# Three subtractions on GpSimd, written in a loop of their own that follows the arrival of batch 2's x

## The chip, the core and the metric

The kernel runs on one core of one Trainium2 chip. The metric is the device time of one execution in microseconds. The kernel before took 658.3 us (median of three runs, 654.86 to 660.84). The profile is of one further execution.

## The reference

All is in float32. Batches B = 4, heads H = 12, sequence S = 448, head size D = 64.

```
scores = q @ k.T / sqrt(64) - log(448)
attn   = sigmoid(scores)
x      = (attn @ v), heads side by side        # 1792 x 768
y      = ((x @ w_a) * (x @ w_b)) @ w_out       # 1792 x 1536, then 1792 x 768
logits = y @ phi                               # 8 experts of 4 slots
d      = softmax of logits over the tokens     # slot_input = d.T @ y
per expert: relu(slot_input @ w1) @ w2
out    = softmax of logits over the slots @ slot_out
```

## The kernel before, in words

**Attention** goes by pairs of heads, six to a batch: pair g is pair g % 6 of batch g // 6 (batches are counted from 0), 24 in all. For a pair VectorE (DVE) turns k and q, rounds each to a high part and subtracts that for a low part (`emit_TK`: transpose, cast, subtraction for k, then the same three for q; L205, L197, L198). TensorE (PE) makes the scores from these parts (L260: high by high, high by low, low by high), ScalarE (ACT) the sigmoid (L266), PE the product with v (L288, L294, L301), and ACT or DVE copies the result out as x of the pair (L323), `xt[g]`. From pair 14 on the pairs are finished two by two: the x of 14 and 15 are copied out one after the other, then those of 16 and 17.

**The first expert layer** is x @ w_a times x @ w_b. Batch 0 and batch 3 go by `ab`. Batches 1 and 2 go together as the two block rows of a Strassen product (Winograd's form, `unit`, L879): A11 and A12 are the first and last three x tiles of batch 1, A21 and A22 those of batch 2. For each of the three tiles i the operands are made in place: S3 = A11 - A21 (L800), S1 = A21 + A22 (L801), S2 = A22 - S3 (L802), S4 = A12 - S2 (L807, L812). A11 itself, A12 and S2 are also split into high and low parts (`split_x`, L782, L783). S3, S1, A22 and S4 are split later (`late_operands`), when the attention is over.

**The weights** of these products are read back from DRAM: `load_u(0)` (L737) reads the first block into the tile hp0, `prep_u(0)` makes the weight blocks from it. Its first step, `block(0, 0)`, is a cast on DVE (L754) and a subtraction on GpSimd (POOL, L755); the next ones are four subtractions on POOL (L768, L770).

**What sets the order.** Each engine runs its instructions in the order in which they are written, and the order is made by generators that are advanced by turns. The loop at the end of attention advances `att_g`; at each of its steps it advances `ops = operands()` once. What `operands` yields decides on the weights: if it yields 1 and the x of pair 15 is there, or if it has ended, `prep_u(0)` is advanced by a step:

```
        if next(ops, 0) in ((0, 1) if GQ + 1 in xt else (0,)):
            pu = pu or prep_u(0)
            next(pu, None)
```

`load_u(0)` is written when the x of pair 13 is there. All reads from DRAM go through the queue of SyncE (SP), in order.

Of the kernel before, what the change touches and what calls it, by code (L numbers as in the profile page):

```python
# [14 lines left out]
ALU = mybir.AluOpType  # L15
# [12 lines left out]
NP = H // 2  # L28
# [13 lines left out]
def body(ctx, tc, q, k, v, w_a, w_b, w_out, phi, w1, w2, out):  # L42
    nc = tc.nc
    pe, act, dve, pool, sp = nc.tensor, nc.scalar, nc.vector, nc.gpsimd, nc.sync
# [259 lines left out]
    xt = {}  # L304
# [475 lines left out]
    def split_x(nm, i, t, pl, names, rnd=None, sub=None):  # L780
        xh, xl = (pl.tile([128, S], F32R, tag=x, name=x) for x in names)
        (rnd or dve.tensor_copy)(xh, t)  # L782
        (sub or pool).tensor_tensor(xl, t, xh.bitcast(F32), op=ALU.subtract)  # L783
        xs[nm, i] = xh, xl

    def operands():

        cp, late = pools["cp"], []
        for i in range(3):
            split_x("A11", i, xt[NP + i], cp, (f"A11h{i}", f"A11l{i}"), act.copy)  # L790
            yield
            split_x("A12", i, xt[NP + 3 + i], cp, (f"A12h{i}", f"A12l{i}"), act.copy)
            yield
        for i in range(3):
            while 2 * NP + 3 + i not in xt:
                yield 1
            yield
            a11, a12, a21, a22 = (xt[n + i] for n in (NP, NP + 3, 2 * NP, 2 * NP + 3))
            s2 = cp.tile([128, S], F32, tag="s2", name="s2", bufs=2)
            pool.tensor_tensor(a11, a11, a21, op=ALU.subtract)  # L800
            pool.tensor_tensor(a21, a21, a22, op=ALU.add)  # L801
            pool.tensor_tensor(s2, a22, a11, op=ALU.subtract)  # L802
            for _ in range(5):
                yield
            split_x("S2", i, s2, cp, (f"S2h{i}", f"S2l{i}"))
            if not i:
                pool.tensor_tensor(a12, a12, s2, op=ALU.subtract)  # L807
            else:
                late.append((a12, s2))
            yield  # L810
        for a12, s2 in late:
            pool.tensor_tensor(a12, a12, s2, op=ALU.subtract)  # L812
# [391 lines left out]
    for kk in range(NP):  # L1204
# [6 lines left out]
    pools["cp"] = cp_ctx.enter_context(tc.tile_pool(name="cp", bufs=1, side="left"))  # L1211
    run["lsd2"] = (hps_t[0][:, 1536:1536 + S], hps_t[1][:, 1536:1536 + S], hps_t[2][:, 4 * S:4 * S + 128], hps_t[2][:, 4 * S + 128:])
    ops, pu = operands(), None
    then = [(2 * NP + 1, lambda: load_u(0)), (GQ + 5, lambda: reload_gk(0, 1, gk_01[1])),
            (GQ + 6, lambda: load_u(1)), (GQ + 7, lambda: reload_gk(0, 0, gk_01[0])),
# [234 lines left out]
```

## Time and profile before

| | |
|---|---|
| three runs | 658.3 us median, 654.86 to 660.84 |
| profiled execution | 654.76 us, span 652.9 us |
| PE busy | 626.5 us (96%) |
| DVE / ACT / POOL busy | 383.6 / 298.3 / 310.1 us |
| stretch of the change | 215 to 280 us of the span, the last pairs of attention |

Times in rows are microseconds from the span's start, unless marked ns. A row of the timeline gives the start, the duration, the engine, the line, the operation with output and inputs, and in brackets the time that the engine sat idle before it and what ended that. PE's ends are modelled. The granted clock is TensorE's, as a share of full speed.

### The profile page before, as it was taken

How to read it: one execution, taken by the hardware profiler on the slowest of the kernel's cores; microseconds unless marked ns; L12 is line 12 of the kernel's file. 1: busy time of each engine (PE TensorE's matmuls, PEld its weight loads, DVE VectorE, ACT ScalarE, POOL GpSimd, SP SyncE). 2: the span in 40 equal slices, each digit the busy share in tenths (PEclk: the TensorE clock that was granted, in tenths of full speed). 3: DMA queues.
4: the chain of work that ended last, by engine and by line, in shares of the span. 5: the costliest groups of instructions: out<-in, count | busy, mean ns of one | idle time of the engine just before them, and what ended most of it. 6: DMA issues, size and time to landing. Idle time of an engine off the chain costs nothing.

```text
span 652.9 us, 10851 instructions
## 1 busy us (share of the span) xinstructions
PE 626.5 (96%) x3989; PEld 447.6 (69%) x3989; DVE 383.6 (59%) x557; ACT 298.3 (46%) x539; POOL 310.1 (47%) x235
## 2 busy tenths in 40 slices
PE   8999999999999999999999999999999999997685
PEld 5557777777776554489988989887889885441121
DVE  4764877889793789498677776856243323030013
ACT  4988889889875876754423332201110002110012
POOL 0234587777772267379986576553335431000000
PEclk9999999999999999999999999999999999998899
DMA  9999889799878766901314333299899999999998
GB/s 213 268 275 261 274 284 340 260 301 301 256 177 209 139 148 125 276 19 49 97 50 105 102 100 84 71 261 319 230 380 405 392 329 367 419 401 416 410 372 300
DMA packets 148564, 159.76 MB, mean 245 GB/s; under 512 B 73584, under 2 KB 126640, under 8 KB 144432
## 3 DMA queue, kind: packets, MB, share of 16 engines
q1 hardware_dynamic: 145984, 157.35, 77.2%
q10 hardware_dynamic: 2528, 1.72, 0.8%
q8 instruction: 32, 0.52, 0.3%
q14 instruction: 20, 0.16, 0.1%
HBM read 129.11 MB, written 29.93 MB: 244 GB/s over the span
## 4 chain that ended last, share of the span: by engine, by line
PE 74%; DMA 16%; ACT 3%; DVE 3%; issue 2%; SPq 1%; ACTq 0%; POOL 0%; DVEq 0%; POOLq 0%
PE ab L686 24%; PE sc L879 16%; PE ab L879 8%; PE sc L260 6%; PE sc L288 5%; DMA misc<-clog 3%; DMA eb<-in_moe_w 2%; DMA e<-in_moe_w 2%; DMA hp<-in_moe_w 2%; DMA hp<-ab 2%; PE ab L294 2%; ACT a L266 1%; PE ms L600 1%; DMA ea<-in_moe_w 1%; PE ms L213 1%
## 5 line engine op out<-in xcount | busy, mean ns | idle before, releaser
L472 POOL TENSOR_TENSOR w<-gk,cy 128x768 int32<-128x768 int32 x36 | 66.3, 1843 | 70.8 <-DVE gk L460 39.7
L266 ACT ACTIVATE a<-sc,sums 112x448 f32<-112x448 f32 (+1 forms) x149 | 84.1, 649 | 13.1 <-PE sc L260 13.1
L686 PE MATMUL ab<-t,wh 128*128 128x448 f32 x288 | 64.6, 370 | 0.1
L693 ACT COPY misc<-ab 128x448 f32<-128x448 f32 x24 | 12.7, 529 | 100.4 <-PE ab L686 100.4
L686 PEld LDWEIGHTS ab<-t,wh 128*128 128x128 f32 x288 | 53.5, 188 | 6.8 <-issue 1.8
L570 POOL TENSOR_TENSOR wl<-w,wh 128x768 fp32r<-128x768 f32 x24 | 46.2, 1928 | 10.9 <-ACT wh L569 10.9
L570 POOL TENSOR_TENSOR wl<-hp,wh 128x768 fp32r<-128x768 f32 x16 | 29.4, 1840 | 42.2 <-DVE wh L569 15.3
L288 PE MATMUL sc<-a,vn 112*64 112x448 f32 x192 | 38.7, 545 | 0.2 <-ACT a L266 0.2
L696 DVE TENSOR_TENSOR misc<-misc,ab 128x448 f32<-128x448 f32 x24 | 14.7, 611 | 36.6 <-PE ab L686 36.5
L458 DVE TENSOR_SCALAR mf<-gk 128x768 f32<-128x768 f32 x24 | 22.7, 944 | 22.9 <-ACT gk L441 22.9
L686 PE MATMUL ab<-xh,wl 128*128 128x448 f32 x144 | 34.8, 377 | 0.0
L686 PE MATMUL ab<-xh,wh 128*128 128x448 f32 x144 | 34.5, 375 | 0.0
L754 ACT CAST wx<-T 128x384 fp32r<-128x384 f32 x19 | 9.7, 512 | 53.9 <-DVE T L776 35.9
L686 PE MATMUL ab<-t,wl 128*128 128x448 f32 x144 | 34.3, 373 | 0.0
L686 PE MATMUL ab<-xl,wh 128*128 128x448 f32 x144 | 34.0, 371 | 0.0
L1409 DVE COPY o<-sc 128x384 f32<-128x384 f32 x10 | 5.4, 554 | 48.5 <-PE sc L1387 47.4
L260 PE MATMUL sc<-qh,kh 64*112 64x448 f32 (+1 forms) x139 | 32.2, 432 | 1.0 <-ACT qh L197 0.6
L755 POOL TENSOR_TENSOR wx<-hp,wx 128x384 fp32r<-128x384 f32 x27 | 31.6, 1173 | 2.2 <-ACT wx L754 2.1
L686 PEld LDWEIGHTS ab<-xh,wh 128*128 128x128 f32 x144 | 26.0, 188 | 7.3 <-issue 4.7
L686 PEld LDWEIGHTS ab<-xl,wh 128*128 128x128 f32 x144 | 26.4, 188 | 5.5 <-issue 3.5
L686 PEld LDWEIGHTS ab<-t,wl 128*128 128x128 f32 x144 | 26.7, 188 | 5.1 <-issue 2.0
L686 PEld LDWEIGHTS ab<-xh,wl 128*128 128x128 f32 x144 | 25.7, 188 | 5.1 <-issue 1.7
(511 smaller groups left out, 1574.6 us busy)
## 6 DMA issues: line engine op xcount, KB each, us to landing
hp<-ab SPq DMA_DIRECT2D x14, 768.0 KB, 4.5
gk<-gk SPq DMA_DIRECT2D x44, 224.0 KB, 4.3
ab<-w SPq DMA_DIRECT2D x24, 384.0 KB, 6.9
eb<-in_moe_w SPq DMA_DIRECT2D x7, 1024.0 KB, 11.9
ea<-in_moe_w SPq DMA_DIRECT2D x7, 1024.0 KB, 11.6
eb<-in_moe_w SPq DMA_DIRECT2D x7, 768.0 KB, 15.1
ea<-in_moe_w SPq DMA_DIRECT2D x7, 768.0 KB, 15.0
wr_cv<-in_moe_w_a SPq DMA_DIRECT2D x6, 768.0 KB, 7.9
```

The source lines that it names most:

```text
L260: pe.matmul(sc[h], kx[r, cs], qx[r], start=(i == 0), stop=(i == 2))
L266: act.activation(a, sc, AF.Sigmoid, bias=nlog[:n], scale=1.0 / math.sqrt(D))
L288: pe.matmul(pv[64 * h:64 * h + 64], qkv_t["v", g][:, h, c, :], a_t.pop((g, h, c)), start=(c == 0), stop=(c == C - 1))
L294: pe.matmul(pv[64 * h:64 * h + 64], qkv_t["v", g][:, h, c], a_t.pop((g, h, c)), start=(c == 0), stop=False)
L458: dve.tensor_scalar(mf, m, LOW, HIGH, op0=ALU.max, op1=ALU.min)
L472: pool.tensor_tensor(thirds(w), m.bitcast(I32), thirds(cy_t.pop(x)), op=ALU.add)
L570: pool.tensor_tensor(wl, t, wh.bitcast(F32), op=ALU.subtract)
L686: pe.matmul(t, w[:, kk * 128:(kk + 1) * 128], xt[b * NP + kk][xi], start=(s == 0 and kk == 0), stop=(s == 2 and kk == KD - 1))
L693: act.copy(gT_all[n % 5], t)
L696: dve.tensor_tensor(g, g, t, op=ALU.mult)
L755: pool.tensor_tensor(w[:, 1], t, w[:, 0].bitcast(F32), op=ALU.subtract)
L879: pe.matmul(t, w[:, wi, k * 128:(k + 1) * 128], xs[ORDER[m], k][xi], start=(s == 0 and k == 0), stop=(s == 2 and k == 2))
```

## The change

The subtraction S3 = A11 - A21 is taken out of the loop over the three row blocks and written in a loop ahead of it. That loop waits for the x of pairs 12, 13 and 14, one per turn, where the loop behind it waits for pairs 15, 16 and 17. The new loop yields 1 while it waits and after each subtraction.

```
         for i in range(3):
+            while 2 * NP + i not in xt:
+                yield 1
+            pool.tensor_tensor(xt[NP + i], xt[NP + i], xt[2 * NP + i], op=ALU.subtract)
+            yield 1
+        for i in range(3):
             while 2 * NP + 3 + i not in xt:
                 yield 1
             yield
             a11, a12, a21, a22 = (xt[n + i] for n in (NP, NP + 3, 2 * NP, 2 * NP + 3))
             s2 = cp.tile([128, S], F32, tag="s2", name="s2", bufs=2)
-            pool.tensor_tensor(a11, a11, a21, op=ALU.subtract)
             pool.tensor_tensor(a21, a21, a22, op=ALU.add)
             pool.tensor_tensor(s2, a22, a11, op=ALU.subtract)
```

PE, ACT and SP keep their order. On POOL, at the end of the splits of A11 and A12, there stood before (t0 to t2 are the A11 tiles, hp2 holds A21, misc A22, hp0 the weights):

```order
L800 TENSOR_TENSOR t0_964<-t0_964,hp2_2474 128x448
L801 TENSOR_TENSOR hp2_2474<-hp2_2474,misc_95 128x448
L802 TENSOR_TENSOR s2_2857<-misc_95,t0_964 128x448
L783 TENSOR_TENSOR S2l0_2928<-s2_2857,S2h0_2927 128x448
L807 TENSOR_TENSOR t3_1791<-t3_1791,s2_2857 128x448
L755 TENSOR_TENSOR wl0_2947<-hp0_2472,wl0_2947 128x384
```

and now:

```order
L797 TENSOR_TENSOR t0_964<-t0_964,hp2_2474 128x448
L797 TENSOR_TENSOR t1_1231<-t1_1231,hp2_2474 128x448
L797 TENSOR_TENSOR t2_1513<-t2_1513,hp2_2474 128x448
L755 TENSOR_TENSOR wl0_2851<-hp0_2472,wl0_2851 128x384
L805 TENSOR_TENSOR hp2_2474<-hp2_2474,misc_95 128x448
L806 TENSOR_TENSOR s2_2878<-misc_95,t0_964 128x448
L783 TENSOR_TENSOR S2l0_2948<-s2_2878,S2h0_2947 128x448
L811 TENSOR_TENSOR t3_1791<-t3_1791,s2_2878 128x448
```

The three differences stand together, and the weight subtraction of `block(0, 0)` has moved from behind S4 to a place ahead of S1.

On DVE, from the copy of pair 15's x on, there stood before (kn and qn are k and q of pair 18, then of pair 19):

```order
L323 COPY misc_95<-ab_2829 128x448
L205 STREAM_TRANSPOSE kn_2646<-kn_2646 128x448
L197 CAST kh_2874<-kn_2646 128x448
L198 TENSOR_TENSOR kl_2875<-kn_2646,kh_2874 128x448
L205 STREAM_TRANSPOSE qn_2656<-qn_2656 128x448
L197 CAST qh_2886<-qn_2656 128x448
L198 TENSOR_TENSOR ql_2887<-qn_2656,qh_2886 128x448
L782 CAST S2h0_2927<-s2_2857 128x448
L754 CAST wl0_2947<-hp0_2472 128x384
L205 STREAM_TRANSPOSE kn_2726<-kn_2726 128x448
```

and now:

```order
L323 COPY misc_95<-ab_2831 128x448
L754 CAST wl0_2851<-hp0_2472 128x384
L205 STREAM_TRANSPOSE kn_2647<-kn_2647 128x448
L197 CAST kh_2882<-kn_2647 128x448
L198 TENSOR_TENSOR kl_2883<-kn_2647,kh_2882 128x448
L205 STREAM_TRANSPOSE qn_2657<-qn_2657 128x448
L197 CAST qh_2894<-qn_2657 128x448
L198 TENSOR_TENSOR ql_2895<-qn_2657,qh_2894 128x448
L782 CAST S2h0_2947<-s2_2878 128x448
L205 STREAM_TRANSPOSE kn_2728<-kn_2728 128x448
```

The cast of the first weight block has moved from behind the six steps of pair 18 to a place ahead of them. The reason is in the yields: by the time of the third subtraction the x of pair 15 is there, so the 1 that follows it advances `prep_u(0)` by its first step.

## Rows read from the trace of the kernel before

**Rows 1.** Page, part 4: the chain that ended last, share by engine.

```profile
PE 74%; DMA 16%; ACT 3%; DVE 3%; issue 2%; SPq 1%; ACTq 0%; POOL 0%; DVEq 0%; POOLq 0%
```

**Rows 2.** Windows: us, busy of each engine, granted clock, DMA share, GB/s.

```profile
275.00:300.00 25.00, 25.00 (x211) 21.01 (x208) 20.19 (x26) 13.54 (x31) 18.08 (x15) 1.00 0.16 50
```

**Rows 3.** Waits of PE, 225 to 653 us: in total, times, longest.

```profile
PE ms L260 <- DVE ql L198: 0.6, 1, 0.6
PE ms L260 <- DVE qh L197: 0.4, 1, 0.4
```

**Rows 4.** Timeline of POOL.

```profile
215.12 1.14 POOL L800 TENSOR_TENSOR t<-t,hp 128x448 f32<-128x448 f32 x1
...
230.76 1.16 POOL L801 TENSOR_TENSOR hp<-hp,misc 128x448 f32<-128x448 f32 x1 [14.50 <-DVE misc L323]
231.88 1.30 POOL L802 TENSOR_TENSOR s<-misc,t 128x448 f32<-128x448 f32 x1
...
238.01 1.15 POOL L755 TENSOR_TENSOR wl<-hp,wl 128x384 fp32r<-128x384 f32 x1
...
256.54 2.79 POOL L812 TENSOR_TENSOR t<-t,s 128x448 f32<-128x448 f32 x2
```

**Rows 5.** Timeline of PE.

```profile
235.72 0.37 PE L260 MATMUL ms<-qh,kh 64*128 64x448 f32 x2
...
236.13 0.37 PE L260 MATMUL ms<-ql,kh 64*128 64x448 f32 x2
...
247.20 0.54 PE L260 MATMUL ms<-qh,kh 64*128 64x448 f32 x2 [0.18 <-ACT a L266]
...
248.60 0.54 PE L260 MATMUL ms<-ql,kh 64*128 64x448 f32 x2 [0.65 <-DVE ql L198]
...
259.73 0.54 PE L260 MATMUL ms<-qh,kh 64*128 64x448 f32 x2 [0.35 <-DVE qh L197]
...
260.30 0.53 PE L260 MATMUL ms<-ql,kh 64*128 64x448 f32 x2
...
278.22 0.87 PE L879 MATMUL sc<-S2h,wh 128*128 128x448 f32 x3
```

**Rows 6.** Timeline of SP's queue.

```profile
229.38 0.59 SPq L737 DMA_DIRECT2D hp<-ab  x1
...
449.41 0.87 SPq L1151 DMA_DIRECT2D ea<-out  x1
```

**Rows 7.** Line L737, 215 to 272 us: who waited, and landing.

```profile
  DVE wl L754: 0.3, 1
DMA to landing us min/median/max: 6.5/6.9/7.2
```

**Rows 8.** Timeline of DVE.

```profile
230.00 0.62 DVE L323 COPY misc<-ab 128x448 f32<-128x448 f32 x1 [2.62 <-PE ab L301]
230.54 0.63 DVE L205 STREAM_TRANSPOSE kn<-kn 128x448 f32<-128x448 f32 x1
...
234.68 0.63 DVE L198 TENSOR_TENSOR ql<-qn,qh 128x448 fp32r<-128x448 f32 x1
...
235.92 1.13 DVE L754 CAST wl<-hp 128x384 fp32r<-128x384 f32 x1 [0.31 <-DMA hp<-ab]
236.97 0.63 DVE L205 STREAM_TRANSPOSE kn<-kn 128x448 f32<-128x448 f32 x1
...
242.88 0.65 DVE L205 STREAM_TRANSPOSE kn<-kn 128x448 f32<-128x448 f32 x1 [0.25 <-DMA kn<-in_k]
...
247.09 1.45 DVE L198 TENSOR_TENSOR ql<-gk,qh 128x448 fp32r<-128x448 f32 x1
...
265.99 0.35 DVE L754 CAST wl<-hp 128x384 fp32r<-128x384 f32 x1
```

**Rows 9.** Windows in the last stretch, columns as in rows 2.

```profile
592.20:595.50 3.30, 1.36 (x6) 0.14 (x2) 0.00 (x0) 0.00 (x0) 0.00 (x0) 1.00 1.03 420
595.50:598.80 3.30, 2.75 (x14) 0.57 (x18) 0.00 (x0) 0.00 (x0) 0.00 (x0) 0.53 1.01 411
```

More of the change, by code (lines that the diff above doesn't have):

```diff
@@ L794, in operands @@
         for i in range(3):
+            while 2 * NP + i not in xt:
+                yield 1
+            pool.tensor_tensor(xt[NP + i], xt[NP + i], xt[2 * NP + i], op=ALU.subtract)
+            yield 1
+        for i in range(3):
             while 2 * NP + 3 + i not in xt:
@@ L799, in operands @@
             s2 = cp.tile([128, S], F32, tag="s2", name="s2", bufs=2)
-            pool.tensor_tensor(a11, a11, a21, op=ALU.subtract)
             pool.tensor_tensor(a21, a21, a22, op=ALU.add)
```

## The prediction, made before the changed kernel ran

> **What bounds the kernel now.** I read the chain of waits first: it is PE for 74% and DMA for 16% of the span [rows 1]. The DMA share lies in the last stretch, where expert weights stream in; the change is far ahead of it. The windows come second: right behind the change, where the Strassen products run, PE is busy 25.00 of 25 us [rows 2]. Here the reader should see that a microsecond which PE loses ahead of 275 us has nowhere to be made up in that stage. Then the waits of PE: between 225 us and the products it waits only in the scores of two pairs, for DVE's q parts [rows 3], 0.65 and 0.35 us, with 0.18 us for ACT ahead of the first [rows 5]. So near the change the bound is PE, with DVE close behind it, and POOL far from it. POOL ends its operand work at 256.54 + 2.79 = 259.33 [rows 4], and the first product that reads an S2 starts at 278.22 [rows 5], 18.9 us later. An earlier end of that work is worth nothing by itself.
>
> **The change part by part.**
>
> *The three differences.* As many instructions as before. The first already ran at 215.12, behind the splits, and POOL then stood for 14.50 us [rows 4]; its place in POOL's order is unchanged. The second and third go into that idle time and into the time until the cast below. Each is about 1.14 us [rows 4], and it is taken out of the time behind the cast below, in which POOL runs beside DVE. On the path they cost nothing; the cover is POOL's idle time, and were that gone, the 18.9 us of slack behind it. What they may give is a share of the waits of PE for DVE; it is in the last term.
>
> *The weight block's cast.* This is the part that matters. The new loop's third yield is a 1, and the x of pair 15 is there by then, so DVE's cast of hp0 is written directly behind the copy of x 15, ahead of the six steps that make k and q of pair 18. The cast reads what SP fetches at 229.38 [rows 6], 6.5 us to landing [rows 7], which is 235.9; in the profile it starts at 235.92, after DVE had already waited 0.31 us for that very transfer [rows 8]. SP's order is unchanged and the read is issued from there, so it lands at the same moment in the new kernel. DVE then finishes the copy at 230.62 and stands until 235.92. Queued behind the cast are pair 18's six steps, then S2's cast, then pair 19's. On POOL the subtraction of this block waits for the cast too, and S1 and S2 of the first block behind it; they have the slack named above. ACT has a short copy of pair 18's k in its order, which needs only the first of the six steps; its sigmoids behind it are late, but PE is later.
>
> The cast itself is short when POOL stands: 0.35 us against 1.13 beside POOL [rows 8]. Pair 18's steps therefore begin at 235.92 + 0.35 = 236.27 in place of 230.54. They took 234.68 + 0.63 - 230.54 = 4.77 us, with POOL beside them from 230.76 to 231.88 + 1.30 = 233.18 [rows 4, 8]. Pair 20's, with POOL beside them all the time, took 247.09 + 1.45 - 242.88 = 5.66 [rows 8]. In the new order POOL has three operations beside pair 18's, 1.15 + 1.16 + 1.30 = 3.6 us [rows 4] in place of two. Between 4.77 and 5.66 I take 4.9, nearer the row of the same pair. They end at 241.17. PE's first scores of pair 18 stand at 235.72, and it takes the low part of q at 236.13 [rows 5], 0.82 us after it was ready. Now it gets it at 241.17: PE is late by 241.17 - 236.13 = **5.0 us** (4.9 to 5.8 by the two ends).
>
> *TensorE's clock.* The nearest row for what follows such a stand is in the last stretch: after 3.30 us with 1.36 busy, the granted clock of the next 3.30 us was 0.53 [rows 9], so the work ran at 1.2 GHz for most of them in place of 2.4. Here PE does nothing at all for about 4.5 us before the score matmuls go on. I take it that the clock falls: 3.30 x 0.47 = **1.5 us** more in a stretch where PE always has work. The ends are 0 (the clock holds) and 1.55.
>
> The Trainium skill (TensorE: Matmul & The Clock Gate, Part 1: The HAM clock gate) says that an idle array is put back to 1.2 GHz and gets 2.4 GHz again only after it was kept busy. By that rule the sum holds the 1.5 us; by the short waits of this stretch alone, at which the clock stayed full, it would not. The last stretch of this trace [rows 9] agrees with the page.
>
> *What is won back.* PE's later waits are for DVE, and DVE has less to do there: the cast and its wait (0.31 + 1.13 us [rows 8]) are gone from behind pair 18, and the 0.25 us for k of pair 20 [rows 8] too, since that transfer is long in. From 235.72 to 236.13, undisturbed, the two steps take 0.41 us; from 247.20 to 248.60 they took 1.40, and 0.18 us stood ahead [rows 5]: 0.99 + 0.18 = 1.17 us lost. From 259.73 to 260.30 it is 0.57, so 0.16 + 0.35 = 0.51 [rows 5]. Together 1.7 us; with PE late and slow I take all of it as won back (**-1.7 us**); with none, 0.
>
> *The sum.* 5.0 + 1.5 - 1.7 = **+4.8 us**. Behind that, PE's work and the loads are paced alike: the first expert load is issued at 449.41 [rows 6], by steps that PE's products set, so the shift is carried to the end. Against the profiled execution (654.76 us) that is 659.6. This execution lies 3.5 us under the median of the three runs, 658.3, and against the median the sum is **663.1 us**.
>
> **Rivals.**
>
> 1. *The clock holds.* Then the 1.5 us are not paid, but PE meets DVE sooner and wins back only about 1.2 of the 1.7: 5.0 - 1.2 = +3.8, so 662.1. For it: PE ran through short waits at full clock here. Against it: [rows 9], with PE at least partly busy before the fall.
>
> 2. *Nothing is won back and pair 18 is slow.* 5.8 + 1.5 = +7.3, so 665.6. DVE stays as far behind as PE, so that the two later waits stay where they are. For it: DVE's six steps beside POOL need 5.66 us, and PE's pairs follow each other at (247.20 - 235.72) / 2 = 5.7 [rows 5]. Against it: DVE loses 1.4 us of work in just that place.
>
> 3. *Faster: the read is there in time.* Each microsecond by which hp0 lands sooner than 235.92 takes one off PE's stand; from 235.92 - 5.0 = 230.9 on there is none. Then only the relief is left: DVE runs pair 20's and 22's steps with two POOL operations fewer beside them and PE gets back up to 1.7 us, 656.6. For it: nothing in SP's order forbids a quicker transfer. Against it: 6.5 us is the shortest of the two reads of this line in this stretch [rows 7], and it would have to take 1.5.
>
> 4. *The stand is there, but the end does not move.* The last stretch waits for DMA; if the weight stream began at its old time, PE's lateness would be taken up in waits there: +0, 658.3. Against it: 449.41 [rows 6] is a step in PE's program, and PE is full up to it [rows 2].
>
> 5. *The change does less than it says.* For the first of the three differences that is so: nothing moves. It changes neither sum nor chance.
>
> **Chances.** Forecast 0.50, the clock holds 0.17, nothing won back 0.15, the end does not move 0.10, faster 0.06; 0.02 for what I do not see. About 1% is what three runs of this kernel can tell, since those shown lie 0.9% apart. 1% of 658.3 is 6.6 us, so that the forecast (+0.7%) counts as no change unless the runs scatter upwards. Slower by over 1% holds most of rival 2 and a quarter of the forecast, 0.25; faster by over 1% would need 6.6 us that no part gives, 0.03; within 1% is 0.72. The range goes from 656 (rival 3, and the end that does not move) to 668 (rival 2 with the scatter of the runs): it leaves out about 2 in 10.
>
> **What would show it.** In the new profile: on DVE the cast from hp0 straight behind the copy of pair 15's x, with some 5 us idle before it, ended by the read of hp0; pair 18's steps ending near 241; on PE one wait for DVE's q part of pair 18, about 4.5 to 5 us, the longest of attention, and a low granted clock in the 3 us behind it; the waits of 0.65 and 0.35 us gone; the first product of S2, 278.22 before [rows 5], near 283. On POOL the second and third difference near 219 and 231. I am wrong if DVE's idle time before the cast is under 1 us, if PE does not wait there, or if the products begin late and the end does not.

## The result and the profile after

The changed kernel took 659.95 us (median of 21 runs, 657.73 to 664.57), the kernel before 657.05 us (21 runs, 653.82 to 660.84). The ratio is 1.0053, 95% interval 1.0039 to 1.0066: slower by 3.5 us (2.6 to 4.3), inside 1%. The prediction was 663.1 us against 658.3, which is +4.8; range 656 to 668. The profiled execution has a span of 658.1 us against 652.9.

DVE after the copy of pair 15's x, columns as in [rows 8], which it answers:

```profile
230.75 0.62 DVE L323 COPY misc<-ab 128x448 f32<-128x448 f32 x1 [2.53 <-PE ab L301]
236.01 0.36 DVE L754 CAST wl<-hp 128x384 fp32r<-128x384 f32 x1 [4.64 <-DMA hp<-ab]
236.29 0.64 DVE L205 STREAM_TRANSPOSE kn<-kn 128x448 f32<-128x448 f32 x1
...
240.44 0.63 DVE L198 TENSOR_TENSOR ql<-qn,qh 128x448 fp32r<-128x448 f32 x1
240.98 0.39 DVE L782 CAST S2h<-s 128x448 fp32r<-128x448 f32 x1
241.28 0.64 DVE L205 STREAM_TRANSPOSE kn<-kn 128x448 f32<-128x448 f32 x1
...
252.58 0.62 DVE L198 TENSOR_TENSOR ql<-gk,qh 128x448 fp32r<-128x448 f32 x1
```

The cast stands behind the copy and waits 4.64 us for its read, where it waited 0.31. Pair 18's six steps come after it. The last row is the low part of q of pair 20, which took 1.45 us before [rows 8]. PE, the answer to [rows 5]:

```profile
240.55 0.54 PE L260 MATMUL ms<-qh,kh 64*128 64x448 f32 x2 [3.92 <-DVE qh L197]
240.91 0.39 PE L260 MATMUL ms<-qh,kl 64*128 64x448 f32 x2
241.12 0.54 PE L260 MATMUL ms<-ql,kh 64*128 64x448 f32 x2
241.59 1.77 PE L275 MATMUL sc<-gk,kr 64*64 64x448 f32 x8
243.29 3.27 PE L294 MATMUL ab<-a,gk 128*64 128x448 f32 x12
...
247.40 0.55 PE L260 MATMUL sc<-qh,kh 64*128 64x448 f32 x2
...
283.15 0.88 PE L883 MATMUL sc<-S2h,wh 128*128 128x448 f32 x3
```

The same products and the next scores in the trace of before:

```profile
236.43 1.22 PE L275 MATMUL sc<-gk,kr 64*64 64x448 f32 x8
237.58 2.48 PE L294 MATMUL ab<-a,gk 128*64 128x448 f32 x12
...
240.95 0.54 PE L260 MATMUL sc<-qh,kh 64*128 64x448 f32 x2
```

The one wait of 3.92 us is the only one that PE has from 225 to 300 us; the three of before (0.65, 0.35, 0.18) are gone. The products behind it are slow. The windows show why (stretch, busy of PE, PEld, DVE, ACT, POOL, then the granted clock, DMA share, GB/s):

```profile
241.00:245.00 4.00, 4.00 (x20) 1.25 (x18) 3.83 (x7) 2.46 (x5) 3.55 (x3) 0.57 0.68 131
245.00:246.00 1.00, 1.00 (x8) 0.31 (x6) 0.97 (x2) 0.00 (x0) 0.92 (x2) 1.00 0.44 74
```

After PE's stand the granted clock averaged 0.57 for four microseconds, most of them at 1.2 GHz in place of 2.4, and then it was full again.

POOL, the answer to [rows 4]:

```profile
215.96 1.15 POOL L797 TENSOR_TENSOR t<-t,hp 128x448 f32<-128x448 f32 x1
220.19 1.15 POOL L797 TENSOR_TENSOR t<-t,hp 128x448 f32<-128x448 f32 x1 [3.08 <-ACT hp L323]
231.36 1.16 POOL L797 TENSOR_TENSOR t<-t,hp 128x448 f32<-128x448 f32 x1 [10.01 <-ACT hp L323]
236.45 1.00 POOL L755 TENSOR_TENSOR wl<-hp,wl 128x384 fp32r<-128x384 f32 x1 [3.94 <-DVE wl L754]
```

The differences ran when each x was there, in time that POOL had to spare.

**One measure for all runs.** Executions differ by a microsecond or two ahead of this stretch. So I measure from the start of DVE's copy of pair 15's x to the start of PE's first product of S2: 278.22 - 230.00 = 48.22 us before [rows 5, 8], and 283.15 - 230.75 = **52.40** after, +4.18. From that product to the end of the span it is 652.9 - 278.22 = 374.68 and 658.1 - 283.15 = 374.95. The loss is made in the stretch and carried to the end.

Each stretch below is that of one traced execution. How much it varies was not measured, except that e3 and e8, the same kernel twice, differ by 0.14 us. In the eight traces of the experiments the part behind it took 373.6 to 375.8 us, so a microsecond in the stretch need not show in the total.

### The profile page after: what moved, and what is told of

Read it like the earlier page. It is cut to its first block, busy times and chain, and to the rows that moved or that the text cites. A ratio compares the mean times of both kernels' runs of the same rounds, so it can differ in the third digit from the quotient of the medians.

```text
span 658.1 us, 10850 instructions
## 1 busy us (share of the span) xinstructions
PE 629.8 (96%) x3989; PEld 449.4 (68%) x3989; DVE 381.4 (58%) x557; ACT 298.2 (45%) x539; POOL 310.0 (47%) x235
## 4 chain that ended last, share of the span: by engine, by line
PE 76%; DMA 13%; ACT 5%; DVE 3%; issue 1%; SPq 1%; ACTq 0%; POOL 0%; POOLq 0%; DVEq 0%
PE ab L686 24%; PE sc L883 16%; PE ab L883 8%; PE sc L260 6%; PE sc L288 4%; PE ab L294 3%; DMA misc<-clog 3%; DMA eb<-in_moe_w 2%; DMA e<-in_moe_w 2%; DMA hp<-in_moe_w 2%; ACT a L266 2%; DMA ea<-in_moe_w 1%; PE ms L213 1%; DMA ab<-w 1%; PE ms L600 1%; PE sc L275 1%
```

## The experiments

Theory: the cast at the head of DVE's queue, with its data late, is the whole loss. Rivals: the differences' new place costs; or the cast costs wherever its data is; or POOL's order does it.

| run | copy, product | stretch | against before | ratio, 95% interval |
|---|---|---|---|---|
| before | 230.00, 278.22 | 48.22 | | |
| the change | 230.75, 283.15 | 52.40 | +4.18 | 1.0053 (1.0039 to 1.0066) |
| e1, differences alone | 230.91, 277.98 | 47.07 | -1.15 | 1.0000 (0.9978 to 1.0022) |
| e2, cast early | 231.38, 285.60 | 54.22 | +6.00 | 1.0105 (1.0075 to 1.0135) |
| e3, change, early read | 231.83, 278.68 | 46.85 | -1.37 | 0.9978 (0.9951 to 1.0006) |
| e4, before, early read | 232.43, 280.60 | 48.17 | -0.05 | 1.0005 (0.9984 to 1.0026) |
| e5, change, PE kept busy | 231.92, 281.87 | 49.95 | +1.73 | 1.0045 (1.0027 to 1.0063) |
| e6, change, cast on POOL | 231.88, 281.47 | 49.59 | +1.37 | 1.0030 (1.0010 to 1.0051) |
| e7, differences, early read | 230.28, 276.94 | 46.66 | -1.56 | 0.9966 (0.9945 to 0.9986) |
| e8, as e3 | 230.42, 277.13 | 46.71 | -1.51 | 0.9972 (0.9949 to 0.9995) |

**e1, the differences alone** (against the changed kernel)

```
             pool.tensor_tensor(xt[NP + i], xt[NP + i], xt[2 * NP + i], op=ALU.subtract)
-            yield 1
+            if i < 2:
+                yield
```

> The three differences stand together as in the change, and the weight block's cast and subtraction stand where they stood before (the new loop's last yield is left out, the others give nothing that advances the weights). If the cast is what costs (theory): no wait of PE near 236 us, DVE's cast at about 236 as before, and a time between that of the kernel before and 1.7 us less (ratio 0.997 to 1.000), since POOL runs two operations fewer beside pairs 20 and 22. If the differences' new place costs by itself (rival): a ratio near 1.005.

The cast is back behind S2's:

```profile
235.70 0.63 DVE L198 TENSOR_TENSOR ql<-qn,qh 128x448 fp32r<-128x448 f32 x1
236.24 0.39 DVE L782 CAST S2h<-s 128x448 fp32r<-128x448 f32 x1
236.54 0.36 DVE L754 CAST wl<-hp 128x384 fp32r<-128x384 f32 x1
```

In the stretch PE has one wait left, 0.25 us for ACT, and the stretch is 1.15 us shorter. In the total that doesn't show: 1.0000, with an interval of 1.4 us to each side. The differences don't cost.

**e2, the cast early without the new loop** (against the kernel before)

```
             while 2 * NP + 3 + i not in xt:
                 yield 1
+            if not i:
+                yield 1
             yield
```

> The kernel before with one more turn that yields 1 ahead of the first row block: the cast and the subtraction of the first weight block stand early as in the change, the differences stay where they were. Theory: the whole loss is here: DVE idle some 4 to 5 us ahead of the cast, PE waiting about 4 us for pair 18's q part, a granted clock of about 0.5 behind that, ratio 1.004 to 1.008, perhaps a little more than the change since POOL has nothing taken off it later. Rival (the differences cost): ratio 1.000.

One more `yield 1` in the kernel before gives the whole loss and more: +6.00 us in the stretch, 6.9 us in the total (4.9 to 8.8). DVE, then PE, then POOL:

```profile
236.64 0.36 DVE L754 CAST wl<-hp 128x384 fp32r<-128x384 f32 x1 [4.63 <-DMA hp<-ab]
...
241.07 1.44 DVE L198 TENSOR_TENSOR ql<-qn,qh 128x448 fp32r<-128x448 f32 x1
```

```profile
241.18 0.54 PE L260 MATMUL ms<-qh,kh 64*128 64x448 f32 x2 [3.91 <-DVE qh L197]
...
242.56 0.74 PE L260 MATMUL ms<-ql,kh 64*128 64x448 f32 x2 [0.55 <-DVE ql L198]
243.23 1.77 PE L275 MATMUL sc<-gk,kr 64*64 64x448 f32 x8
244.93 4.23 PE L294 MATMUL ab<-a,gk 128*64 128x448 f32 x12
```

```profile
237.08 1.00 POOL L755 TENSOR_TENSOR wl<-hp,wl 128x384 fp32r<-128x384 f32 x1 [20.43 <-DVE wl L754]
238.03 1.28 POOL L802 TENSOR_TENSOR t<-t,hp 128x448 f32<-128x448 f32 x1
...
240.75 1.28 POOL L804 TENSOR_TENSOR s<-misc,t 128x448 f32<-128x448 f32 x1
```

DVE's wait is the same as after the change. What is worse is the low part of q, 1.44 us against 0.63, with POOL still busy beside it (1.28 us from 240.75). That comes of this edit. Contrary to the expectation it also moves the first difference: the weight subtraction is now written ahead of that difference, which so runs at 238.03, behind the late read. It runs at 215.12 before the change [rows 4] and at 215.96 after it. PE waits 0.55 us more. And the clock stayed low longer, although PE had work:

```profile
242.00:248.00 6.00, 5.45 (x21) 1.62 (x22) 5.79 (x8) 2.46 (x5) 4.98 (x6) 0.50 0.61 113
248.00:249.00 1.00, 1.00 (x6) 0.21 (x2) 0.20 (x1) 0.00 (x0) 1.00 (x1) 0.75 0.69 110
```

So the 54.22 - 52.40 = 1.8 us by which e2 is worse than the change can't be put down to the cast alone: the late first difference is in them. What e2 shows is the stand, 3.91 us of PE behind 4.63 us of DVE, without the new loop.

**e3 and e8, the change with the read one pair earlier**

```
-    then = [(2 * NP + 1, lambda: load_u(0)), (GQ + 5, lambda: reload_gk(0, 1, gk_01[1])),
+    then = [(2 * NP, lambda: load_u(0)), (GQ + 5, lambda: reload_gk(0, 1, gk_01[1])),
```

> The changed kernel with the read of the first weight block issued when the x of pair 12 is there, one pair sooner. Theory (the cast costs because its data is late): the cast runs at about 231 us without waiting for a transfer, PE waits under 0.3 us for pair 18, and the loss is gone: ratio to the kernel before 0.996 to 1.000, below 1 by what the cast no longer takes behind pair 18 (0.31 + 1.13 us) and PE's waits of 0.65 and 0.35 us. Rival (the cast's and POOL's place costs whatever the data does, or the read disturbs the loads of k and q): ratio 1.002 or more.

> The changed kernel with the read one pair earlier once more, beside the others on one chip, to narrow its interval: 0.9978 [0.9951, 1.0006] before. From pair 15's copy to S2's first product it took 46.85 us against 48.22, which is 1.4 us or a ratio of 0.998; if that is carried to the end the ratio comes out between 0.996 and 0.999, if it is lost in the last stretch's waits for transfers, at 1.000.

DVE in e3:

```profile
231.83 0.62 DVE L323 COPY misc<-ab 128x448 f32<-128x448 f32 x1 [2.53 <-PE ab L301]
232.37 0.35 DVE L754 CAST wl<-hp 128x384 fp32r<-128x384 f32 x1
232.64 0.64 DVE L205 STREAM_TRANSPOSE kn<-kn 128x448 f32<-128x448 f32 x1
```

SP issued the read at 219.34 and it landed 5.3 us later; the cast has the same place as after the change and waits for nothing. PE waits for nothing from 200 to 300 us, and the stretch is 1.37 us shorter than before (1.51 in e8). The ratios are 0.9978 and 0.9972, the second below 1 by its interval. The cast's early place costs only while its data is late. POOL keeps the order of the change here, with the weight subtraction ahead of the sums, so that order alone doesn't cost either.

**e4, the kernel before with the earlier read** (the same line changed in it)

> The kernel before with that earlier read alone, as a control for the read's own effect on the queue. Theory: 0.31 us of DVE's wait goes, nothing else; ratio 0.998 to 1.001. If the read disturbs the k and q loads behind it in the queue: over 1.002, and e3 then is to be read against this one.

48.17 us, 1.0005: the read's place in the queue gives or costs nothing that shows. PE's two waits for DVE are gone, and a new one of 0.71 us for ACT, at pair 22, is in their place. DVE:

```profile
237.95 0.35 DVE L754 CAST wl<-hp 128x384 fp32r<-128x384 f32 x1
...
250.84 0.39 DVE L782 CAST S2h<-s 128x448 fp32r<-128x448 f32 x1 [1.04 <-POOL s L802]
```

The cast no longer waits and is short, 0.35 us, and PE's value products (L294) behind pair 20's scores start 1.1 us sooner (251.29 - 232.43 = 18.86 us behind the copy, 249.97 - 230.00 = 19.97 before). By pair 22 that is lost again. On the way DVE waited 1.04 us for POOL's sum for S2, which stands behind a difference (L800, 1.53 us from 246.54).

**e5, the change with PE kept busy**

```
     def emit_S(g, chunks):
+        if g == 3 * NP and 0 in chunks:
+            spin(5)
+            spin(5)
+            run["ms"] -= 2
```

> The changed kernel with ten 128x128 matmuls of no use on PE ahead of pair 18's first scores, in the place where PE stands. In the changed kernel PE waited there 3.92 us, the granted clock was 0.50 from 242 to 244 us, and the score and value products behind it took 1.77 and 3.27 us where the kernel before has 1.22 and 2.48. Theory (the stand brings the clock down, and that costs some 1.4 us of its own): the wait is filled in part, the clock stays near 1.00, those products take their old times, and from the copy of pair 15's x to the first product of S2 it is some 51 us in place of 52.4 (before 48.2); ratio to the kernel before 1.002 to 1.005. Rival (the clock is no part of the loss, DVE comes late again and takes it back): 52.4 us still.

`spin` is the kernel's own warming loop; what it writes is not used. PE:

```profile
238.09 2.50 PE L116 MATMUL ms<-wa 128*128 128x128 f32 x20 [0.28 <-ACT a L270]
240.89 0.54 PE L264 MATMUL ms<-qh,kh 64*128 64x448 f32 x2 [0.30 <-DVE qh L197]
...
241.92 0.98 PE L279 MATMUL sc<-gk,kr 64*64 64x448 f32 x8
242.84 2.48 PE L298 MATMUL ab<-a,gk 128*64 128x448 f32 x12
```

```profile
242.00:248.00 6.00, 6.00 (x46) 2.96 (x46) 5.79 (x8) 3.69 (x8) 5.83 (x5) 1.00 0.62 116
```

The clock stayed full, and the two groups of products took 0.98 and 2.48 us in place of 1.77 and 3.27: the difference is 1.58 us. (The first group takes 0.98 to 1.47 us at the full clock elsewhere in these traces, so its share is the less certain.) The stretch is 52.40 - 49.95 = 2.45 us shorter; the rest of that, some 0.9 us, is the read, after which the cast started 236.31 - 231.92 = 4.39 us behind the copy here and 236.01 - 230.75 = 5.26 after the change. In the total, +3.0 us (1.8 to 4.1) here and +3.5 us (2.6 to 4.3) for the change can't be told apart, so that the clock's part is shown in the trace and not in the median.

**e6, the change with the cast on POOL**

```
-        (act.copy if u else dve.tensor_copy)(w[:, 0], t)
+        (act.copy if u else dve.tensor_copy if m else pool.tensor_copy)(w[:, 0], t)
```

> The changed kernel with the first weight block's cast on POOL in place of DVE, at the same point, so that DVE's queue no longer holds the late read. If POOL's part has 18.9 us of slack, as the prediction said: no wait of PE over 0.5 us at pair 18 or 19, and the loss is gone, ratio 0.997 to 1.001. Rival (POOL too holds something for DVE: S2's cast stands in DVE's queue ahead of pair 19 and needs POOL's sums, which now come behind the late read): PE's wait moves from pair 18 to pair 19 and is 3 to 5 us again, ratio 1.004 to 1.008.

DVE, then POOL, then PE:

```profile
235.57 0.62 DVE L198 TENSOR_TENSOR ql<-qn,qh 128x448 fp32r<-128x448 f32 x1
240.92 0.39 DVE L782 CAST S2h<-s 128x448 fp32r<-128x448 f32 x1 [4.72 <-POOL s L806]
```

```profile
237.10 0.51 POOL L754 CAST wl<-hp 128x384 fp32r<-128x384 f32 x1 [3.45 <-DMA hp<-ab]
```

```profile
243.79 1.50 PE L301 MATMUL ab<-a,gk 64*64 64x448 f32 x8 [1.84 <-ACT a L266]
```

Pair 18 is in time now, but the wait went on along another way. POOL waits 3.45 us for the read, its sums for S2 come behind that, DVE waits 4.72 us for them with pair 19's steps queued behind, ACT waits for the first of these (its copy of pair 19's k), and PE waits 1.84 us for ACT, and 0.51 us for DVE at pair 20. The ratio is 1.0030 (1.0010 to 1.0051), 2.0 us: neither expectation was met; the rival's way, by S2's cast and pair 19's steps, was right, and its 3 to 5 us too much. PE's shorter stand didn't bring the clock down: the granted clock was 1.00 from 242 to 246 us.

**e7, the differences and the earlier read, the cast at its old place** (e1's lines with e3's)

> The three differences together, the cast at its old place (as in the run of the differences alone), and the read one pair earlier. It tells apart what the run with the early read gains from the cast's early place and what from the differences. If the differences give all of it: from pair 15's copy to the first product of S2 47.0 us (48.2 before), ratio 0.997 to 1.000, the same as with the cast early. If the cast's early place has a part of its own: 47.5 us or more.

46.66 us against 46.85 and 46.71 with the cast early: the differences with the early read give all of the gain, and the cast's early place has no part of its own that shows. With the same read but the differences at their old place (e4) there is no gain. The ratio of 0.9966 (0.9945 to 0.9986) is the lowest of all: 2.2 us faster than the kernel before (0.9 to 3.6). It can't be told from e8.

## Why the prediction was right

- *What bounds.* Right: what PE lost ahead of 275 us reached the end (374.95 us behind it against 374.68). The rows named for that [rows 2] reach only to 300 us; the trace of before has PE busy 174.40 of 174.40 us from 275 to 449.4, where the first expert load is issued. Rival 4 (the end does not move) is out.
- *The cast.* Right in mechanism and place; e2 gives the stand without the new loop, e1 none with the cast at its old place, and e3 and e8 none with the cast early and its data there. The term was 5.0 us. Measured against the copy of pair 15's x, PE took pair 18's low part of q at 241.12 - 230.75 = 10.37 in place of 236.13 - 230.00 = 6.13: **4.2 us**. The working had the read land 6.5 us after its issue; it took 5.7, and 236.01 came 5.26 us behind the copy where 5.92 was reckoned. In the six traces that issue the read at this place it took 5.3 to 6.5 us, and the working had taken the longest of them as fixed. Pair 18's steps took 240.44 + 0.63 - 236.29 = 4.78 us; 4.9 was reckoned. PE's own wait was announced as 4.5 to 5 us and took 3.92.
- *The clock.* Right, 1.5 us reckoned: the next scores, behind the slow products, started at 247.40 - 230.75 = 16.65 us behind the copy; in the trace of before the same scores stand at 240.95, which is 10.95 behind it. Of these 5.70 us 4.24 are the stand, which leaves **1.5 us**. Rival 1 (the clock holds) is out, in the trace of this execution.
- *Won back.* 1.7 us reckoned; 5.70 at that point and 4.18 at the first product of S2 leave **1.5 us**. All three waits are gone. Rival 2 (nothing won back) is out. The size was right, the reason only in part: the working put the gain on the cast and its wait, gone from behind pair 18. e4 has the cast short and without a wait, and what it gains at pair 20 is lost by pair 22; e7, with the cast at its old place but the differences moved, keeps 1.56 us. So the gain holds only with the differences out of the way.
- *The sum.* 4.8 us reckoned, 4.2 in the profile, 3.5 by the ratio of the runs (2.6 to 4.3). The term that was too large is the stand, by the time of one transfer.
- *Faster, with the read in time* was not what happened, but e3 shows its condition: with the read landed, the same order of work is 1.4 us faster in the stretch.
- *What was wrong.* The sentence that POOL's part behind the cast has 18.9 us of slack. That is its distance to PE's product. The nearer one who waits is DVE's cast of S2, with pair 19's steps behind it; e6 shows 4.72 us of wait there. It did no harm to the sum, because DVE was as late itself: POOL's sum was there at 238.65 + 1.51 = 240.16, and DVE began that cast at 240.98.

## What to carry to other kernels

An instruction that is moved up a queue takes its data's arrival with it: look at when the read lands, and at what then stands behind the waiting instruction, before looking at what the move frees. Slack has to be counted to the first who waits for a result in any engine's queue, and not to the product at the end. In an order made by generators, a yield is a move: here a turn meant for pacing placed a cast of 0.36 us where it cost 4 us, and the three subtractions with the read one pair sooner are the version that gains, by about 0.3%.

## What was not expected of the hardware

- The low clock did not last equally long. After a stand of PE of 3.92 us it was full again from 245 us on, some 4 us later; in e2, after 3.91 us and a further wait of 0.55, it was 0.50 from 242 to 248 us, with PE busy for 5.45 of these 6, and 4.23 us went into products that take 2.48. What sets that is open.
- The same read of 768 KB took 6.5, 5.7, 6.0, 5.6, 5.3 and 5.5 us from issue to landing in the traces of before, after, e1, e2, e5 and e6, and, issued a pair earlier, 5.3, 5.3, 6.3 and 5.4 us in e3, e4, e7 and e8. Where a late read sets the loss, that alone moves it by a microsecond.
